# Attention and mixer on one core: the first block's relu and square in single tiles, relus of batch 0 on two engines, the last output tile in two column halves

## The chip, the cores and the metric

The kernel runs on one core of a Trainium2 chip. The metric is the device time of one execution in microseconds (us). A core has engines that run side by side and wait for each other through semaphores: TensorE (PE in the profile; its weight loads are listed as PEld), VectorE (DVE), ScalarE (ACT), GpSimd (POOL) and SyncE (SP), whose queue issues DMAs. Matmuls write to PSUM, in banks of 128 partitions x 512 columns of f32.

## The reference

For each of 8 batches, with 3008 tokens (S) and 256 channels:

```python
scores = (1.0 / S) * np.matmul(z, z.transpose(0, 2, 1))     # z: 8 x 3008 x 64
attn = np.maximum(scores, 0.0) ** 2
x = u * np.matmul(attn, v)                                  # u, v: 8 x 3008 x 256
h = np.maximum(x.transpose(0, 2, 1) @ w_tok1, 0.0) @ w_tok2 # 3008 -> 256 -> 3008
y = x + h.transpose(0, 2, 1)
out = y + np.maximum(y @ w_ch1, 0.0) @ w_ch2                # 256 -> 1536 -> 256
```

Every input is f32 and the output is f32; the kernel multiplies in bf16.

## The kernel before, in words

**Tiles.** Tokens are cut into 24 tiles of 128 (the last holds 64) and into six groups of four tiles, 512 tokens each (`QW`, `GK`; the last group has 448). For batch b, a block of queries q (512 tokens) and a group of keys g, the scores are made in two units (`pr` 0 and 1) of two key tiles each. `score_run` (L448) issues a unit's two matmuls into one pair of PSUM banks. `relu` (L480) scales and clips the pair on ScalarE and writes bf16 into a tile `at` (128 x 4 x 512), `square` (L509) squares it in place on VectorE. The product with v, attn @ v, accumulates over all key groups into `acc`, once for each half of the channels (`dh` 0 and 1).

**The first query block of batch 0** (`blk.whole`, q = 0) is done by `whole_matmul` (L596, matmuls at L609) with all 128 rows in one matmul; all other blocks go by `av_matmul` (L692) as two matmuls of 64 rows that run side by side. `grain` (L431) says in how many key tiles at a time a block is handed on: for the first two groups of (b, q) = (0, 0) a pair is used as soon as its square is done, through the events in `early`; later groups wait for all four tiles, through `blocks`.

**The ring.** Scores, turns and most other results share three pairs of PSUM banks (`RING = 3`; `take_slot`, `ring`). A slot comes back when its reader, for scores the relu, is done. In the first block `first_acc` (L358) keeps two further banks for the two sums.

**The planner.** The order of all engines' instructions is worked out when the kernel is built. A loop (L1743) keeps its own clock for TensorE (`pe[0]`) and for ScalarE, VectorE and SP (`free`). `push` (L364) queues an operation on an engine with the time when it is ready, the time that it keeps the engine busy, and the time after which its result counts; `run_engines` (L383) emits them in the order of their start. TensorE's next work is picked among scores, products with v and mixer pieces. While the first block is going and TensorE would have to wait, L1832 puts one matmul on zeros (`fill`, L202, L205) into each 0.22 of the planner's time. What is emitted is static: on the chip each engine keeps that order and waits where a result is late.

**The start** (L1532 on). z of batch 0 comes in f32 by six DMAs on SP and ScalarE's queues, v's first group by POOL (L223). Seven matmuls on zeros are issued, then for the first two groups of z VectorE casts (L178), TensorE turns four tiles by a matmul with the identity (L184) and ScalarE copies them out (L1716). POOL's next loads of v wait for the second of these copies (`after`, L124). One more matmul on zeros follows, and the planner's clocks are set by hand (5.3 for TensorE) before the first two units are scored. Groups 2 and 3 of z are turned by DMA (L150), 4 and 5 later on TensorE (`late_z`, L1638), as is the first group of u (`first_u`).

**The mixer** of a batch follows in pieces: token products (`tok1`, `tok2`), the first channel product (`ch1`, L1143, with relus at L1182 and L1184), and the second by seven products of a Strassen-like scheme (`product`, L1280) or plainly (`ch2`, L1366). **The end**: for the last group of the last batch `ch2` handles one tile at a time, in the order tile 2, the joint tile of two batches' last 64 rows, tile 0, tile 1. Each has 12 matmuls of 256 columns, then `residual` adds on VectorE (L1401), and SP issues the output DMA (L1404).

Of the kernel before, what the change touches and what calls it, by code (L numbers as in the profile page):

```python
# [57 lines left out]
def kernel(  # L58
# [143 lines left out]
    def fill(n, bank):  # L202

        for _ in range(n):
            nc.tensor.matmul(  # L205
                bank, zero[:, :P], zero[:], start=True, stop=True, skip_group_check=True)
# [157 lines left out]
    def push(engine, ready, busy, lat, fn, first=0, room=(), done=None, frees=()):  # L364
        op = Op(ready, busy, lat, fn, first, room, done, frees)
        waiting[engine].append(op)
        return op.done
# [62 lines left out]

    def grain(b, q, g):  # L431

        return 2 if b + q == 0 and g < 2 else GK
    turned = {}

    def can_score(first_unit, most):
# [11 lines left out]
    def score_run(us, start):  # L448
        for unit in us:
            (b, q, g), pr = unit  # L450
            zT = zTs[b].rearrange("p t s -> p (t s)")
            W = widths[q]
            slot, free_at = take_slot()
            begin = max(start, free_at, known(turned[b, q], turned[b, g]))
            cost = column_time(W)
            if triangle(b, q, g):

                cost = (column_time(QW), column_time(P))[pr]
            begin, start = on_pe(begin, "half", cost)
            sc = bank_pair(slot, "sc")  # L460
            for r, i, c0, c1 in parts(unit):
                k = z_tile(b, r, g * GK + i) * P
                m = z_tile(b, r, q * GK) * P
                h = slice(r * d_qk, (r + 1) * d_qk)
                nc.tensor.matmul(  # L465
                    sc[:, r, c0:c1], zT[h, k:k + P], zT[h, m + c0:m + c1],
                    start=True, stop=True)
            if pr == 0:
                live["at"] += 1
                at_free.pop(0)  # L470
            busy = 0.92
            if triangle(b, q, g):
                busy = (0.87, 0.43)[pr]
            if grain(b, q, g) < GK and pr == 0:
                early[b, q, g] = [Done() for _ in range(GK)]
            done = push("act", begin + cost + 0.21, busy, busy + 0.16,
                        lambda t, unit=unit, sc=sc: relu(unit, sc, t))
            ring.append((done, slot))

    def relu(unit, sc, t):  # L480
        (b, q, g), pr = unit
        W = widths[q]
        if pr == 0:
            ats[b, q, g] = sb.tile([P, GK * QW], BF16, tag="at", name="at", bufs=ROOM["at"])
            ready_at[b, q, g] = []
        at = ats[b, q, g]
        pair = slice(2 * pr, 2 * pr + 2)
        if triangle(b, q, g):
            a3 = at.rearrange("p (i w) -> p i w", w=QW)
            for r, i, c0, c1 in parts(unit):  # L490
                nc.scalar.activation(  # L491
                    a3[:, i, c0:c1], sc[:, r, c0:c1], ACT.Relu, scale=inv_S)
            push("dve", t, (0.62, 0.36)[pr], (0.76, 0.5)[pr],
                 lambda t: square_triangle(unit, t))
            return
        if flips(b, q, g):

            view = at.rearrange("p (j i s) -> p j i s", i=GK, s=P)[:, :, pair, :]
            sv = sc.rearrange("p i (j s) -> p j i s", s=P)
        else:  # L500
            view = at.rearrange("p (i w) -> p i w", w=QW)[:, pair, :W]
            sv = sc[:, :, :W]
        nc.scalar.activation(view, sv, ACT.Relu, scale=inv_S)  # L503
        ready_at[b, q, g].append(
            push("dve", t, 0.61, 0.75, lambda t: square(unit, view, t)))

    blocks = {}

    def square(unit, view, t):  # L509
        (b, q, g), pr = unit  # L510
        nc.vector.tensor_mul(view, view, view)  # L511
        if (b, q, g) in early:
            for e in early[b, q, g][2 * pr:2 * pr + 2]:
                e.t = t
            if pr == 0:
                blocks[b, q, g] = (
                    Done(t), ats[b, q, g].rearrange("p (i w) -> p i w", w=QW), "at", [1])
            else:
                ats.pop((b, q, g))
            return  # L520
        if pr < GK // 2 - 1:
            return
        at = ats.pop((b, q, g))
        uses = [1]
        if flips(b, q, g):
            uses[0] = 2
            attn = at.rearrange("p (j i s) -> p i j s", i=GK, s=P)
            done = push("sp", t, 2.2, 6.5, lambda t: flip(b, q, g, at, uses, done),
                        frees=fl_free,
                        room=lambda: has_room(("fl",)) and (  # L530
                            b < 2 or q or turned_back[b - 1] > 1))
        else:
            attn = at.rearrange("p (i w) -> p i w", w=QW)
        blocks[b, q, g] = (Done(t), attn, "at", uses)
        recent[0] = at[:, :1]
# [463 lines left out]
    def add_mixer(b):  # L999
# [347 lines left out]
        def fast(q):  # L1347

            return (b > 0 or q >= HALF) and (b, q) != (B - 1, NQ - 1)

        def ch2(q, half, i, end):
            apart = alone(q, half)
            if i == 0 or apart:
                st["o_slot"], _ = take_slot()
                st["op"] = bank_pair(st["o_slot"], "op")[:, 0, :].rearrange(
                    "p (i d) -> p i d", d=D)
# [79 lines left out]
        def alone(q, half):  # L1436

            return pieces_of(q, half) == 1 or (b, q, half) == (B - 1, NQ - 1, 0)
# [269 lines left out]
    for k, item in enumerate(items):  # L1708
        at_group(begin + k * (NQ * NG - NG - begin + 1 + W_LATER) // len(items), item)

    fill(7, bank_pair(0, "wp")[:, 0, :])

    for c in range(DT):
        zp = first_acc(c).rearrange("p (t s) -> p t s", s=P)
# [6 lines left out]
    load_u(0, 1)  # L1721
    for c in range(DT, GK):
        turn_first_z(c)
    fill(1, bank_pair(0, "wp")[:, 0, :])
    for c, t in enumerate([5.3, 5.9, 9.0, 10.0]):
        turned[0, c] = Done(t)
    pe[0] = 5.3
    free.update(act=5.75, dve=5.0, sp=7.0)
    score_run(units[:2], 5.3)
    late_z(4, 7.8)  # L1730
    late_z(5, 9.0)
    first_u(18.5)
# [152 lines left out]
```

## Time and profile before

| what | us |
|---|---|
| three runs, median (lowest, highest) | 1116.48 (1116.16, 1121.13) |
| the profiled execution's own time | 1116.06 |
| its span, first to last instruction | 1114.0 |
| TensorE busy, of the span | 1108.1 |
| VectorE, ScalarE, GpSimd busy | 780.5, 655.1, 162.7 |
| 8.3 to 24 us: VectorE, ScalarE busy, of 15.7 | 12.38, 14.23 |
| 24 to 60 us: VectorE, ScalarE busy, of 36 | 30.85, 34.82 |
| 60 to 100 us: VectorE, ScalarE busy, of 40 | 37.33, 36.80 |

The profile is one execution; its durations are compared with its own time, 1116.06, and that lies 0.4 below the median of the three runs. Matmuls overlap, and their ends are modelled: a single matmul of 512 columns is listed with 0.38 us, while a row of them start 0.22 apart. So the chain of waits, which goes from start to start, is the better measure of TensorE's time. In timeline lines, the first number is the start in us from the beginning of the span, the second the length of the merged group; in brackets stands the idle time before it and what ended it. "SPq" lines are issues of DMAs, not the transfers.

### The profile page before, as it was taken

The page shows a single profiled execution, that of the slowest core. Times are in us where ns is not written, and L with a number is a line of the kernel's source. Part 1 is how long each engine was busy: PE and PEld are TensorE (multiplying, and loading weights), DVE is VectorE, ACT ScalarE, POOL GpSimd, SP SyncE. Part 2 cuts the span into 40 slices and gives each one's busy share as a digit, 9 for nine tenths or more (in the row PEclk, how much of TensorE's full clock was granted, in tenths as well). Part 3 has the DMA queues.
Part 4 walks back from the last instruction along what each step waited for, and adds up shares of the span by engine and source line. Part 5 has one row for each costly group of instructions (what it writes and reads, how often), then busy time and mean ns, then how long its engine had stood idle before and what let it go on. Part 6 is the DMA issues. An engine that isn't in the chain of part 4 may idle for free.

```text
span 1114.0 us, 26933 instructions
## 1 busy us (share of the span) xinstructions
PE 1108.1 (99%) x10965; PEld 675.6 (61%) x10965; DVE 780.5 (70%) x1855; ACT 655.1 (59%) x817; POOL 162.7 (15%) x382
## 2 busy tenths in 40 slices
PE   9999999999999999999999999999999999999998
PEld 3444574666557665576555865557655576556676
DVE  6889846875758757588566885578756787557775
ACT  8999524645854458545675356653666536743354
POOL 5321100211003110031000311003200120000000
PEclk9999999999999999999999999999999999999999
DMA  9999955796987979779597897868968678585213
GB/s 178 173 183 157 208 117 114 124 179 135 183 137 142 187 126 185 142 141 209 128 174 132 143 197 144 168 121 158 191 156 172 109 157 174 128 160 99 63 58 95
DMA packets 466155, 165.51 MB, mean 149 GB/s; under 512 B 433072, under 2 KB 449008, under 8 KB 466032
## 3 DMA queue, kind: packets, MB, share of 16 engines
q1 hardware_dynamic: 436640, 131.11, 58.0%
q0 software_dynamic: 28880, 32.32, 20.6%
q8 instruction: 85, 1.39, 0.5%
q10 hardware_dynamic: 512, 0.38, 0.1%
q14 instruction: 38, 0.31, 0.1%
HBM read 65.40 MB, written 24.64 MB: 81 GB/s over the span
## 4 chain that ended last, share of the span: by engine, by line
PE 97%; DVE 1%; ACT 1%; issue 1%; POOL 0%; DVEq 0%; POOLq 0%; ACTq 0%
PE acc L692 41%; PE hp L1143 21%; PE xb L1280 10%; PE zb L1280 7%; PE sc L465 6%; PE h_ps L1086 4%; PE a_ps L1029 3%; PE op L1366 3%; PE first_acc L609 1%; DVE a_f L1045 0%; ACT h2pre L1182 0%; PE wp L205 0%; ACT at L503 0%; POOL hs L1156 0%; DVE at L511 0%
## 5 line engine op out<-in xcount | busy, mean ns | idle before, releaser
L1182 ACT ACTIVATE h2pre<-hp 128x1024 bf16<-128x1024 f32 (+1 forms) x277 | 269.4, 1007 | 257.8 <-PE hp L1143 165.3
L692 PEld LDWEIGHTS <-v_sb 64*128 64x128 bf16 x4418 | 238.0, 94 | 219.3
L692 PE MATMUL acc<-at,v_sb 64*128 64x512 bf16 (+1 forms) x2738 | 338.8, 374 | 0.0
L503 ACT ACTIVATE at<-sc 128x1024 bf16<-128x1024 f32 (+1 forms) x290 | 287.5, 1027 | 72.2 <-PE sc L465 65.4
L511 DVE TENSOR_TENSOR at<-at 128x1024 bf16<-128x1024 bf16 (+1 forms) x290 | 198.5, 687 | 110.7 <-ACT at L503 106.7
L1143 PE MATMUL hp<-xT,w_ch_sb 128*128 128x512 bf16 (+1 forms) x1152 | 273.5, 375 | 0.1
L692 PE MATMUL acc<-fl,v_sb 64*128 64x512 bf16 (+1 forms) x1680 | 191.4, 367 | 0.0
L1143 PEld LDWEIGHTS <-w_ch_sb 128*128 128x128 bf16 x1152 | 106.2, 98 | 99.8 <-issue 3.0
L465 PE MATMUL sc<-zT 64*128 64x512 bf16 (+1 forms) x732 | 131.3, 360 | 0.1
L1280 PEld LDWEIGHTS <-hsum 128*128 128x128 bf16 x1944 | 115.9, 98 | 17.6 <-issue 1.1
L1280 PEld LDWEIGHTS <-h2pre 128*128 128x128 bf16 x1458 | 89.1, 98 | 19.3 <-issue 1.2
L820 ACT COPY cp<-acc 128x512 f32<-128x512 f32 (+1 forms) x94 | 54.9, 584 | 71.4 <-PE acc L692 59.8
L826 DVE TENSOR_TENSOR cp<-acc,cp 128x512 f32<-128x512 f32 (+1 forms) x94 | 63.5, 675 | 42.3 <-ACT cp L820 41.8
L491 ACT ACTIVATE at<-sc 128x512 bf16<-128x512 f32 (+3 forms) x152 | 56.1, 444 | 45.4 <-PE sc L465 45.0
L1223 DVE TENSOR_TENSOR hsum<-h2pre 128x512 bf16<-128x512 bf16 (+1 forms) x132 | 52.2, 400 | 37.7 <-ACT h2pre L1182 35.9
L1280 PE MATMUL xb<-w_mix_sb,hsum 128*128 128x128 bf16 x972 | 68.6, 219 | 0.4 <-DVE ro L1317 0.3
L542 DVE TENSOR_TENSOR at<-at 128x512 bf16<-128x512 bf16 (+3 forms) x152 | 41.5, 321 | 38.3 <-ACT at L491 38.2
L1317 DVE TENSOR_TENSOR ro<-xb,u_sb 128x256 f32<-128x256 f32 (+1 forms) x132 | 52.6, 399 | 21.9 <-PE xb L1280 20.2
L465 PEld LDWEIGHTS <-zT 64*128 64x128 bf16 x732 | 42.0, 94 | 41.8 <-issue 3.8
L124 POOL CAST mark<-at 128x1 f32<-128x1 bf16 x24 | 8.9, 369 | 375.2 <-DVE at L511 375.2
L846 DVE TENSOR_TENSOR xT<-cp,uT 128x512 bf16<-128x512 f32 (+1 forms) x94 | 62.4, 664 | 0.8
L1095 DVE TENSOR_TENSOR xT<-xT,h_ps 128x1024 bf16<-128x1024 bf16 (+1 forms) x48 | 54.6, 1172 | 4.7 <-PE h_ps L1086 4.6
(89 smaller groups left out, 983.0 us busy)
## 6 DMA issues: line engine op xcount, KB each, us to landing
out_dram<-ro SPq DMA_DIRECT2D x37, 512.0 KB, 2.9
v_sb<-in_v_dram POOLq DMA_DIRECT2D x40, 256.0 KB, 4.6
ur<-in_u_dram POOLq DMA_DIRECT2D x40, 256.0 KB, 5.1
w_tok_sb<-in_moe_w_tok_dram POOLq DMA_DIRECT2D x10, 256.0 KB, 10.7
zs<-in_z_dram POOLq DMA_DIRECT2D x35, 64.0 KB, 3.7
at<-at SPq DMA_TRANSPOSE x114, 2.4
out_dram<-ro SPq DMA_DIRECT2D x7, 256.0 KB, 2.2
fl<-at SPq DMA_TRANSPOSE x105, 4.4
```

What stands on the lines that cost most here:

```text
L465: nc.tensor.matmul(sc[:, r, c0:c1], zT[h, k:k + P], zT[h, m + c0:m + c1], start=True, stop=True)
L491: nc.scalar.activation(a3[:, i, c0:c1], sc[:, r, c0:c1], ACT.Relu, scale=inv_S)
L503: nc.scalar.activation(view, sv, ACT.Relu, scale=inv_S)
L511: nc.vector.tensor_mul(view, view, view)
L692: nc.tensor.matmul(o, vs[blk.b, g][rows, i, dh * P:(dh + 1) * P], rhs, start=(dh, h) not in blk.begun, stop=stop, skip_group_check=True)
L820: nc.scalar.copy(cp[:, :W], acc[:, 1, :W])
L826: nc.vector.tensor_add(cp[:, :W], acc[:, 0, :W], cp[:, :W])
L846: nc.vector.tensor_mul(xT[:, dh, :full * P].rearrange("p (t s) -> p t s", s=P), acc[:, :full * P].rearrange("p (t s) -> p t s", s=P), uT[: ...
L1095: nc.vector.tensor_add(to, to, h[:, :, :n * P].rearrange("p h (s t) -> p h t s", t=n))
L1143: nc.tensor.matmul(hps[r % len(hps)][:, r, :W], w_ch1_sb[:, dc, cc * P:(cc + 1) * P], xT[:, dc, :W], start=(dc == 0), stop=(dc == DT - 1))
L1182: nc.scalar.activation(h2[:, :, :W], hp[:, :, :W], ACT.Relu)
L1280: nc.tensor.matmul(to[:, i * P:(i + 1) * P], lhs, weights[:, c2, :], start=(first_use and c2 == 0 and i == 0), stop=(c2 == CHT // 2 - 1), ...
```

## The change

There are three parts. At the start, six matmuls on zeros are issued instead of seven and the single one after the turns is left out; the planner's clocks are set 0.5 lower. For the first key group of the first query block the first pair's relu and square are done in two instructions each, one for each key tile, and the products follow tile by tile (`grain` 1). For batch 0, relus of groups that are handed on whole may go to VectorE, as one multiply-and-max from PSUM, where the planner's queues say that ScalarE would be done later than VectorE with relu and square (0.92 against 1.76). As relus can now change order, `at` is made by whichever pair comes first, and a block is done when both pairs are squared. At the end, tile 1 of the last group is computed in two halves of 128 columns, each with 12 matmuls, a bank of its own, an add and an output DMA.

```diff
@@ -430,7 +430,7 @@
     def grain(b, q, g):
-        return 2 if b + q == 0 and g < 2 else GK
+        return GK if b + q or g > 1 else 1 + g
@@ -473,14 +473,25 @@
             if grain(b, q, g) < GK and pr == 0:
                 early[b, q, g] = [Done() for _ in range(GK)]
-            done = push("act", begin + cost + 0.21, busy, busy + 0.16,
-                        lambda t, unit=unit, sc=sc: relu(unit, sc, t))
+            if grain(b, q, g) == 1 and pr == 0:
+                busy += 0.14
+            ready = begin + cost + 0.21
+            engine = "act"
+            if b == 0 and grain(b, q, g) == GK:
+                def load(e):
+                    return max(free[e], ready) + sum(op.busy for op in waiting[e])
+                if load("act") + 0.92 > load("dve") + 1.76 + ON_DVE:
+                    engine, busy = "dve", 1.15
+            done = push(engine, ready, busy, busy + 0.16,
+                        lambda t, unit=unit, sc=sc, engine=engine: relu(unit, sc, engine, t))
             ring.append((done, slot))
 
-    def relu(unit, sc, t):
+    ON_DVE = 0.0
+
+    def relu(unit, sc, engine, t):
         (b, q, g), pr = unit
         W = widths[q]
-        if pr == 0:
+        if (b, q, g) not in ats:
...
-        nc.scalar.activation(view, sv, ACT.Relu, scale=inv_S)
+        if grain(b, q, g) == 1 and pr == 0:
+            for i in range(2):
+                nc.scalar.activation(view[:, i], sv[:, i], ACT.Relu, scale=inv_S)
+                push("dve", t + 0.5 * (i - 1), 0.34, 0.5,
+                     lambda t, i=i: square_one(unit, view, i, t))
+            return
+        if engine == "act":
+            nc.scalar.activation(view, sv, ACT.Relu, scale=inv_S)
+        else:
+            nc.vector.tensor_scalar(view, sv, inv_S, 0.0, AX.mult, AX.max)
...
+    def square_one(unit, view, i, t):
+        (b, q, g), pr = unit
+        nc.vector.tensor_mul(view[:, i], view[:, i], view[:, i])
+        early[b, q, g][i].t = t
+        if i == 0:
+            blocks[b, q, g] = (
+                Done(t), ats[b, q, g].rearrange("p (i w) -> p i w", w=QW), "at", [1])
...
-        if pr < GK // 2 - 1:
+        squared[b, q, g] = squared.get((b, q, g), 0) + 1
+        if squared[b, q, g] < GK // 2:
             return
@@ -1348,8 +1377,32 @@
+        def last_tile(q, half, i, end):
+
+            res = sb.tile([P, 2, D], F32, tag="fl", name="res", bufs=ROOM["fl"])
+            k = half * 2 + i
+            for h in range(DT):
+                slot, _ = take_slot()
+                op = bank_pair(slot, "op")[:, 0, :P]
+                for cc in range(CHT):
+                    nc.tensor.matmul(
+                        op, st["h2", q, cc // 4][:, cc % 4, k * P:(k + 1) * P],
+                        w_ch2_sb[:, cc, h * P:(h + 1) * P], start=(cc == 0), stop=(cc == CHT - 1))
+
+                def residual(t, h=h, op=op):
+                    nc.vector.tensor_add(res[:, h, :P], op, st["u", q][:, h, k, :])
+                    nc.sync.dma_start(
+                        out=rows_of(out[b], q)[:, k, h * P:(h + 1) * P], in_=res[:, h, :P])
+
+                ring.append((push("dve", end - 0.65 * (1 - h) + 0.21, 0.21, 0.36, residual), slot))
+            done_with_h2(q)
+            release("us", us_uses[q])
+
         def ch2(q, half, i, end):
             apart = alone(q, half)
+            if (b, q, half, i) == (B - 1, NQ - 1, 0, 1):
+                last_tile(q, half, i, end)
+                return
@@ -1708,7 +1761,7 @@
-    fill(7, bank_pair(0, "wp")[:, 0, :])
+    fill(6, bank_pair(0, "wp")[:, 0, :])
...
-    fill(1, bank_pair(0, "wp")[:, 0, :])
-    for c, t in enumerate([5.3, 5.9, 9.0, 10.0]):
+    for c, t in enumerate([4.8, 5.4, 9.0, 10.0]):
         turned[0, c] = Done(t)
-    pe[0] = 5.3
-    free.update(act=5.75, dve=5.0, sp=7.0)
-    score_run(units[:2], 5.3)
+    pe[0] = 4.8
+    free.update(act=5.25, dve=4.5, sp=7.0)
+    score_run(units[:2], 4.8)
```

More of the change, by code (lines that the diff above doesn't have):

```diff
@@ L502, in relu @@
             sv = sc[:, :, :W]
-        nc.scalar.activation(view, sv, ACT.Relu, scale=inv_S)
+        if grain(b, q, g) == 1 and pr == 0:
[8 more added lines that the diff above has]
+            nc.vector.tensor_scalar(view, sv, inv_S, 0.0, AX.mult, AX.max)
         ready_at[b, q, g].append(
             push("dve", t, 0.61, 0.75, lambda t: square(unit, view, t)))
-    blocks = {}
+    blocks, squared = {}, {}
+    def square_one(unit, view, i, t):
[5 more added lines that the diff above has]
+                Done(t), ats[b, q, g].rearrange("p (i w) -> p i w", w=QW), "at", [1])
     def square(unit, view, t):
```

## The prediction

> **What bounds the kernel now.** I read the page first: the span and the engines' busy shares, then the chain that ended last.
>
> ```profile
> span 1114.0 us, 26933 instructions
> ...
> PE 1108.1 (99%) x10965; PEld 675.6 (61%) x10965; DVE 780.5 (70%) x1855; ACT 655.1 (59%) x817; POOL 162.7 (15%) x382
> ...
> PE 97%; DVE 1%; ACT 1%; issue 1%; POOL 0%; DVEq 0%; POOLq 0%; ACTq 0%
> ```
>
> TensorE (PE) is on the chain for 97% of the span. A microsecond is gained only where TensorE waits or works for nothing. The table by windows of 100 us shows 99.64 to 100 us of PE busy from 200 on; between 200 and 1090 its idle time adds up to 1.2 us. What is left lies at the two ends. Next view: the chain in order of time, first 10 us (start, length, what).
>
> ```profile
> 1.20 3.17 PE wp L205 x7
> 4.36 0.85 PE first_acc L184 x8
> 5.21 0.44 PE wp L205
> 5.66 0.04 issue
> 5.70 0.98 PE sc L465 x4
> 6.68 0.75 PE first_acc L205 x3
> 7.43 0.54 PE sc L465 x4
> 7.97 0.54 PE first_acc L205 x2
> 8.51 0.86 PE first_acc L609 x4
> 9.37 0.22 PE zp L184 x4
> ```
>
> L205 is a matmul on zeros. Seven stand ahead of the first turns of z, one behind them, and five (3 and 2) pass time until the first product with v (L609) can start, at 8.35 by the timeline. From there the chain is useful matmuls without a gap. The third view is the timeline of the other engines at that place.
>
> ```profile
> 6.35 1.02 ACT L503 ACTIVATE at<-sc 128x1024 bf16<-128x1024 f32 x1 [0.45 <-PE sc L465]
> ...
> 7.40 0.69 DVE L511 TENSOR_TENSOR at<-at 128x1024 bf16<-128x1024 bf16 x1 [2.67 <-ACT at L503]
> ...
> 10.81 0.23 PEld L609 LDWEIGHTS <-v_sb 128*128 128x128 bf16 x2 [0.21 <-DMA v_sb<-in_v_dram]
> ```
>
> The first L609 waits for relu (6.35 to 7.37) and square (7.40 to 8.09). At 10.81 PE's weight load waits for a load of v. The last view is the timeline of SP and VectorE at the end (SP's lines are DMA issues).
>
> ```profile
> 1108.45 0.33 SPq L1404 DMA_DIRECT2D out_dram<-res  x1
> 1108.88 0.51 SPq L1404 DMA_DIRECT2D out_dram<-res  x1
> 1109.48 0.54 SPq L1404 DMA_DIRECT2D out_dram<-res  x1
> 1110.12 0.54 SPq L1404 DMA_DIRECT2D out_dram<-res  x1
> 1111.07 0.34 SPq L1404 DMA_DIRECT2D out_dram<-res  x1
> ...
> 1110.62 0.42 DVE L1401 TENSOR_TENSOR res<-op,u_sb 128x256 f32<-128x256 f32 x1 [0.89 <-PE op L1366]
> ```
>
> The last matmul ends at 1110.58, its residual at 1111.04, the last DMA is issued at 1111.07 and takes 1.7 us to land.
>
> **Part 1, two matmuls on zeros fewer.** A zero matmul ahead of 6 us takes 3.17 minus its tail over 7: starts lie 0.43 apart. Six end at 1.20 + 6 x 0.43 = 3.76. The first turn then waits for the cast of z (3.29 plus 0.43) and a weight load of 0.10, so it starts at 3.88, not 4.16: 0.28 earlier. The eighth zero matmul (0.44) lay beside ScalarE's cast (4.83, 0.58), for which the scores wait at 5.57; taking it away gains nothing by itself. The scores start at 5.42 instead of 5.70. What is late next is ScalarE's cast, and then the relu: 6.07 instead of 6.35.
>
> **Part 2, relu and square tile by tile.** By the nearest rows a 128x512 relu takes 0.60 (L491), two 128x512 casts in a row start 0.48 apart (L1716), and a 128x512 square takes 0.42 (L542). So tile 0 is squared at 6.07 + 0.60 + 0.03 + 0.42 = 7.12, tile 1 at about 7.57. Two instructions instead of one cost ScalarE 2 x 0.48 against 0.92 from relu to relu, at least 0.04, at most the 0.14 that the planner books. But the first v, issued at 1.43, takes 6.3 us to land: 7.73. No product can start earlier. Nor does the order let it: in the planner's own clock (4.80 + 0.095 + two scores = 5.33) the next two scores can go when the first bank is nearly free, at 6.22, so (6.22 - 5.33)/0.22 gives four zero matmuls between, where there were three; the two behind the second pair of scores go. TensorE then runs: scores to 6.3, zeros to 7.35, a change of shape (0.1, as 0.54 for four scores against 0.43), scores to 7.88, 0.1, first product at 7.98. That is 0.37 ahead of 8.35.
>
> The lead isn't kept whole. After the eight matmuls of the first block, one turn of z and two more scores TensorE comes to the second v at about 10.65. It now lands at 6.08 + 4.7 = 10.8. Its issue on POOL follows ScalarE's second cast, so it moves 0.28 earlier, with four more loads of v behind it on the same queue; if the 4.7 hold it lands at 10.5, and if the queues' traffic holds it at 10.8, the lead ends there. So the start is worth 0 to 0.37; I take **0.3**, since the issue is 0.28 earlier and the row's duration is the only evidence of what follows. Behind the waiting weight load stand the scores of the fourth block and ScalarE for them, which has two relus (about 10.3 to 12.2) to do first, so that wait isn't handed on. The later loads land well ahead of use (the third at about 12.1, used after 13.7). Once TensorE never waits, the lead goes to the end unchanged.
>
> **Part 3, relus on VectorE.** Such a relu has no row with a multiply; the nearest is L1184, 128x1024 from PSUM, 1.22 on VectorE, against 1.03 on ScalarE. The rule takes VectorE when ScalarE's queue plus 0.92 exceeds VectorE's plus 1.76; of three scores issued together the third can qualify. It shortens no wait of TensorE, since there is none in batch 0 after 8.35. What it may cost is cover: in 8.3 to 24 VectorE is busy 12.38 of 15.70, and three such relus (3.67) would bring it to 16.05, 0.35 over; in 24 to 60 there is room for four (30.85 of 36), in 60 to 100 for two (37.33 of 40). The rule compares queues, so a full VectorE gets none, and finished blocks ahead of TensorE cover a late one. Value 0, bounds -0.4 (a bank freed sooner saves two changes of shape of 0.1 each, twice) and +0.35.
>
> **Part 4, the last tile in halves.** TensorE: 24 matmuls of 128 columns for 12 of 256. L1280's twelve take 0.67 on the chain, so 1.34 for 1.31: +0.03. VectorE's last add is 128x128: 0.29 (L1317) for 0.42: -0.13. But SP now issues two DMAs where there was one. The fourth issue ends at 1110.66; half 0 is ready at 1109.11 + 0.67 + 0.2 + 0.3 = 1110.3 and stands right behind it, from about 1110.72. The three issues that stood directly behind another took 0.51 to 0.54, the two that didn't 0.33 and 0.34. Half 1, ready at 1110.96, is therefore issued at 1111.12 to 1111.35, not 1111.07, and its own issue may take 0.2 more. Landing follows: 1.7 for 128 KB here and 2.0 for 64 KB of 64 rows, so half the bytes save 0.1 at most. Bounds -0.05 and +0.5; I take **+0.25**, towards the rows of issues that queue.
>
> **Sum.** -0.3 + 0 + 0.25 = -0.05. The profiled execution took 1116.06 (span 1114.0 and 2.1 around it); the three other runs have a median of 1116.48 (1116.16 to 1121.13). I forecast against the median: **1116.4**, which is no change. A measurement of this kernel tells about 0.5% (5.6 us) from no change.
>
> [...] The rows first: zero matmuls start 0.43 apart up to 6 us and 0.22 apart from 6.6 on; turns of z take 0.85 for eight at 4.36 and 0.22 for four at 9.37. TensorE runs at half pace for its first 5 us, though the granted clock of that window reads 1.00. [...]
>
> **Rivals.**
> - *The fast pace comes late (slower).* Place: TensorE now idles from 4.73 to 5.42, 0.7 us, where it idled 0.3 (5.44 to 5.70). By the rows the fast pace came some 5.1 us after the first matmul (1.20 to 6.3). If the longer gap starts that count afresh at 5.42, it comes at 10.5, and the matmuls from 6.3 on do in 4.2 us the work of 2.1. The four zeros are in it and only pass time ahead of v at 7.73, which absorbs about 0.5. Price 1.6: **1118.0**. It decides when the scores at 7.4 still start 0.43 apart. For it: the gap is new and longer. Against: TensorE is still busy for most of 1.2 to 6.3. Chance 0.12. [...]
> - *The second v lands early and the order has fewer gaps (faster).* The lead of 0.37 stays whole, batches of scores save 0.4 in changes of shape, SP's issues take 0.34 (end +0.05) and some of the later 1.2 us of idling goes: -0.35 - 0.4 + 0.05 - 0.4 = -1.1, **1115.4**. For it: relus on VectorE free banks sooner, and the whole later order is planned anew. Chance 0.25.
> - *VectorE or the new order costs more (slower).* 0.35 in the first block and as much idling again as the 1.2 us now seen: **1118.0**. The point: squares in 8 to 24 that wait for VectorE and not ScalarE, with L609 behind them. Chance 0.13.
> - *The VectorE branch is never taken:* then part 3 is 0 anyway, and the forecast stands.
>
> **How the numbers follow.** The forecast, within 0.6 of 1116.4, has 0.50. To hold the time 8 times in 10 the range takes in most of the three rivals: 1114.7 to 1118.2. All cases lie within 5.6 us of the median; for an order that goes wrong over hundreds of microseconds I leave faster 0.02, same 0.94, slower 0.04.
>
> **What would show it.** Part 1: first turn at 3.88, scores at 5.42, one group of L205 of six. Part 2: relus of 128x512 at 6.07, four zeros behind the first scores, first L609 at about 8.0, and L609 of the second block at 10.5 to 10.8, with PE's weight load waiting for v there. Part 3: some lines of VectorE at<-sc with 128x1024 from f32, no wait of PE for VectorE. Part 4: six L1404-like issues, the last at 1111.1 to 1111.4 less the lead. I'd be wrong if the lead at 24 us were over 0.6 or below 0, if the fast pace came late, or if PE's idle time between 200 and 1090 left 0 to 2.4.

## The result, and the profile after

| | before | after |
|---|---|---|
| median of 22 runs each, us | 1116.59 | 1120.6 |
| lowest, highest | 1115.44, 1121.13 | 1118.05, 1130.78 |
| the profiled execution | 1116.06 | 1121.0 |
| its span | 1114.0 | 1119.1 |

The ratio after to before is 1.0046, with a 95% interval of 1.0029 to 1.0063. A second set of runs gave 1119.3 against 1116.88, ratio 1.0042 (1.0025 to 1.0059). So the change costs 2.4 to 4.0 us by the medians, and some 5 by the ratios, in which the longest runs weigh more. That is within the 0.5% which the prediction called no change, but outside its range, which ended at 1118.2. Nine of the ten longest runs of after have a mean granted clock of 0.998 or lower, as have 11 of the 32 in both sets and 4 of 111 runs of before.

The page of after first: the span, the busy line and the chain that ended last.

```profile
span 1119.1 us, 26955 instructions
...
PE 1109.2 (99%) x10974; PEld 680.1 (61%) x10974; DVE 782.5 (70%) x1858; ACT 654.9 (59%) x817; POOL 161.1 (14%) x382
...
PE 92%; DVE 4%; DMA 2%; ACT 1%; issue 0%; DVEq 0%; ACTq 0%
```

TensorE's share of the chain fell from 97% to 92%; DMA has entered it with 2%, and VectorE has gone from 1% to 4%. The chain in order of time (start, length, what) shows where the DMA comes in.

```profile
1.20 2.74 PE wp L205 x6
...
3.97 0.62 PE first_acc L184 x4
...
4.61 0.59 ACT zT L1769
...
5.25 0.63 PE sc L465 x2
...
5.91 0.11 ACT at L516
6.02 6.49 DMA zT<-zr
...
12.55 0.60 PE sc L465 x4
```

Up to 5.91 this is the start that was forecast: six zeros, the first turn at 3.97, the scores at 5.25. Then a DMA takes the chain for 6.49 us: the second DMA transpose of z (`turn_first_z`, L150), issued at 6.02 and landed at 12.51. In before it was issued at 5.84 and had landed at 10.63. The timeline at that place:

```profile
5.91 1.08 ACT L516 ACTIVATE at<-sc 128x512 bf16<-128x512 f32 x2 [0.22 <-PE sc L465]
6.54 0.91 DVE L531 TENSOR_TENSOR at<-at 128x512 bf16<-128x512 bf16 x2 [1.62 <-ACT at L516]
7.94 1.47 PE L638 MATMUL first_acc<-at,v_sb 128*128 128x512 bf16 x6
...
11.49 0.60 PE L638 MATMUL first_acc<-at,v_sb 128*128 128x512 bf16 x2 [0.78 <-DMA v_sb<-in_v_dram]
12.55 0.60 PE L465 MATMUL sc<-zT 64*128 64x512 bf16 x4 [0.46 <-DMA zT<-zr]
```

The relus in single tiles (L516) and their squares (L531) are in time, and the first product with v (L638, L609 before) starts at 7.94, not 8.35. Then TensorE waits twice, for the second load of v (landed at 11.45, before 10.77) and for the transpose. The two waits take 0.95 and 0.62 out of its row of starts.

To see where the rest comes from, I follow the lag: by how much a landmark that both kernels have (a VectorE gate, a copy out of PSUM) comes later in after than in before, and how much longer than usual the next matmul is in starting.

| where (us in after) | lag added | what TensorE waits for |
|---|---|---|
| up to 8 | -0.4 | nothing; the lead |
| 10.7 to 12.6 | +1.57 | v's second load (0.95), z's transpose (0.62) |
| 8 to 40 | +0.5 | 28 changes between matmuls of 64 and of 128 rows in the first 240 us, 22 in before; starts lie 0.31 apart at a change and 0.22 in a row, so about 0.1 each; one of the six falls into the wait at 12.55 |
| 110.8 | +0.7 | scores: a PSUM bank that ScalarE's relu frees late |
| 132.9 and 150.8 | +0.8 | VectorE (at 150.8 an add, L1436, which had waited 4.3 for an output DMA to land; 3.3 in before) |
| 494, 630, 768 | +0.8 | the sums `hsum`, VectorE |
| behind the last matmul | +1.1 | SP's output DMAs |
| sum | 5.1 | span 1119.1 against 1114.0 |

These are differences of single executions. pe_longer and sp_longer, further down, run before's program up to its end, and yet they lag behind before's trace by 0.2 at 65 us and by 1.5 from 126 us on. So much a trace can differ by itself.

SP's issues at the end of after, which stand against the five of before:

```profile
1112.44 0.33 SPq L1457 DMA_DIRECT2D out_dram<-res  x1
...
1113.47 1.63 SPq L1457 DMA_DIRECT2D out_dram<-res  x1
...
1115.83 0.40 SPq L1394 DMA_DIRECT2D out_dram<-res  x1
...
1114.64 0.29 DVE L1393 TENSOR_TENSOR res<-op,u_sb 128x128 f32<-128x128 f32 x1 [0.38 <-PE op L1388]
```

The third issue, a store of 64x256 that stands ahead of the halves, takes 1.63; the same one took 0.54 in before. The fourth follows at 1115.20, and the halves (L1394) queue behind it: the last result is ready at 1114.93 and its DMA is issued at 1116.32.

### The profile page after: what moved, and what is told of

Same layout as the page of the kernel before. It is cut to its first block, busy times and chain, and to the rows that moved or that the text cites. A ratio compares the mean times of both kernels' runs of the same rounds, so it can differ in the third digit from the quotient of the medians.

```text
span 1119.1 us, 26955 instructions
## 1 busy us (share of the span) xinstructions
PE 1109.2 (99%) x10974; PEld 680.1 (61%) x10974; DVE 782.5 (70%) x1858; ACT 654.9 (59%) x817; POOL 161.1 (14%) x382
## 4 chain that ended last, share of the span: by engine, by line
PE 92%; DVE 4%; DMA 2%; ACT 1%; issue 0%; DVEq 0%; ACTq 0%
PE acc L721 40%; PE hp L1172 20%; PE xb L1309 9%; PE zb L1309 7%; PE sc L465 6%; PE h_ps L1115 4%; PE a_ps L1058 3%; PE op L1419 2%; DMA out_dram<-ro 1%; PE first_acc L638 1%; ACT at L521 1%; DVE at L539 1%; DMA zT<-zr 1%; DVE ro L1346 1%; DVE a_f L1074 0%
## 5 line engine op out<-in xcount | busy, mean ns | idle before, releaser
L721 PEld LDWEIGHTS <-v_sb 64*128 64x128 bf16 x4418 | 243.2, 94 | 214.9 <-issue 0.4
L521 ACT ACTIVATE at<-sc 128x1024 bf16<-128x1024 f32 (+1 forms) x287 | 284.1, 1026 | 74.6 <-PE sc L465 67.3
L1172 PEld LDWEIGHTS <-w_ch_sb 128*128 128x128 bf16 x1152 | 106.1, 98 | 100.7 <-issue 4.2
```

What stands on the lines that cost most here:

```text
L721: nc.tensor.matmul(o, vs[blk.b, g][rows, i, dh * P:(dh + 1) * P], rhs, start=(dh, h) not in blk.begun, stop=stop, skip_group_check=True)
L1172: nc.tensor.matmul(hps[r % len(hps)][:, r, :W], w_ch1_sb[:, dc, cc * P:(cc + 1) * P], xT[:, dc, :W], start=(dc == 0), stop=(dc == DT - 1))
```

## The experiments

**Theory A:** the two zeros fewer let v's second load be issued ahead of z's second transpose, and the two get into each other's way; the rest is the end and changes of shape. **Rivals:** the order of the work, planned anew, costs by itself (B: through the two relus that went to VectorE; C: through any new order); the end is the halves' own doing, or SP's longer queue. Every kernel below has a profile, and its time is compared with before on the same chip. "Lag" is that behind before's trace.

| kernel | median us (runs) | ratio to before, 95% | lag at 65 us | lag at TensorE's end | added behind it |
|---|---|---|---|---|---|
| after, second set | 1119.3 (10) | 1.0042 (1.0025 to 1.0059) | +1.4 | +2.1 | +1.0 |
| v_later | 1119.62 (12) | 1.0028 (1.0007 to 1.0049) | +0.8 | +2.2 | +1.3 |
| v_sooner | 1117.43 (12) | 1.0002 (0.9989 to 1.0015) | +0.6 | +0.4 | 0.0 |
| zeros_alone | 1117.28 (12) | 1.0003 (0.9984 to 1.0022) | +0.8 | +1.2 | 0.0 |
| end_alone | 1117.16 (12) | 1.0000 (0.9983 to 1.0018) | +0.4 | +6.5 | +0.5 |
| tiles_alone | 1116.19 (12) | 1.0006 (0.9992 to 1.0019) | 0.0 | -0.5 | 0.0 |
| no_dve | 1124.84 (6) | 1.0082 (1.0067 to 1.0098) | -0.3 | +3.3 | +1.3 |
| end_undone | 1118.34 (12) | 1.0022 (1.0006 to 1.0038) | +1.3 | +1.7 | 0.0 |
| after_mended | 1117.67 (11) | 1.0012 (0.9996 to 1.0027) | +0.4 | +1.0 | +0.5 |
| tiles_mended | 1118.12 (11) | 1.0007 (0.9996 to 1.0018) | +1.2 | +1.1 | +0.4 |
| relu_on_act | 1120.19 (11) | 1.0033 (1.0015 to 1.0051) | +2.3 | +2.4 | +0.6 |
| pe_longer | 1117.08 (10) | 1.0005 (0.9993 to 1.0017) | +0.2 | -0.2 | +0.5 |
| sp_longer | 1117.93 (1) | | 0.0 | +1.5 | its own load |
| held_whole | 1117.67 (11) | 1.0017 (1.0000 to 1.0034) | +0.5 | +0.7 | 0.0 |

Before had medians of 1116.35 to 1116.88 in these sets.

### The start: four kernels on the loads

**v_later** is after, with a small memset on GpSimd ahead of v's loads; **v_sooner** is before, with v's loads waiting for the first copy of z, not the second; **zeros_alone** is before with two zeros fewer and nothing else; **end_alone** is before with the last tile in halves.

```diff
     after(zTs[0][:, DT * GK - 1, :1])
+    nc.gpsimd.memset(w_tok1_sb[:, 0:2, :], 0.0)        # v_later
```
```diff
-    after(zTs[0][:, DT * GK - 1, :1])                  # v_sooner
+    after(zTs[0][:, GK - 1, :1])
```
```diff
-    fill(7, bank_pair(0, "wp")[:, 0, :])               # zeros_alone
+    fill(6, bank_pair(0, "wp")[:, 0, :])
...
-    fill(1, bank_pair(0, "wp")[:, 0, :])
```

> The changed kernel, with one memset of 128x512 on POOL (of a weight tile that is loaded later) between POOL's wait for ScalarE's second cast and the loads of v, so that the second load of v is issued some 0.4 us later, at about 6.3 us. Theory A (the earlier load of v shares the DMA engines with the two transposes of z that run at the same time, and both land late): the second transpose lands before 11 us instead of 12.5, v at 10.7 to 11.0 instead of 11.45, the scores of the fourth group of keys start at about 11 instead of 12.55; the median falls from 1120.6 to about 1119 and the scatter of 13 us over the runs shrinks to about 3. Rival B (the new order of the matmuls costs the time, not the landings): the median stays within 0.5 of 1120.6.

> The kernel before, with one edit: POOL's loads of v wait for ScalarE's first cast instead of its second, so that the second load of v is issued about 0.4 us sooner (5.6 instead of 6.08); the order of the matmuls is that of before. Theory A: the transposes and the load collide here too; the second transpose lands after 11.5 instead of 10.63, v no sooner than 10.8; the median rises by 1 to 2.5 us to 1117.6 to 1119, with a wider scatter. Rival B: no change, 1116.6 within 0.4, or 0.1 to 0.3 faster since v is there sooner.

> The kernel before with only the two matmuls on zeros taken out (six and none); the planner's clocks and so all other instructions are those of before. The scores start at 5.3 to 5.4. Theory A: v is issued 0.2 to 0.3 us sooner and may collide: between 0 and +2 us, 1116.6 to 1118.6, with some runs high. Prediction: -0.3 to 0. Rival C (the longer gap on TensorE holds its half pace for longer): scores at about 7.1 still start 0.43 apart, +1 us or more in the runs where it happens, with a mean granted clock below 1.000.

> The kernel before with only the last tile in two halves of 128 columns. Theory D (SP's issues stand in a queue and are late): the last issue starts 0.3 to 1.5 us later after the last matmul, the span ends 0.3 to 1.1 us later, median 1116.9 to 1117.7. If the late third issue of the changed kernel's profile (1.63 us) was chance: +0.1 to +0.5. If the halves hide VectorE's add as meant: -0.1.

The landings settle the start. The two issues of before and of after, from the timelines of SP and GpSimd:

```profile
5.84 1.23 SPq L150 DMA_TRANSPOSE zT<-zr  x1
...
6.08 0.76 POOL L223 DMA_DIRECT2D v_sb<-in_v_dram  x1
```
```profile
6.02 1.21 SPq L150 DMA_TRANSPOSE zT<-zr  x1
...
5.87 0.76 POOL L223 DMA_DIRECT2D v_sb<-in_v_dram  x1
```

In before the transpose is issued 0.24 ahead of v, in after 0.14 behind it. Over all sixteen traces (later kernels included):

| kernel | v issued after the transpose by | transpose landed | v landed |
|---|---|---|---|
| v_sooner | -0.60 | 12.26 | 10.30 |
| no_dve | -0.19 | 11.90 | 11.30 |
| zeros_alone | -0.16 | 12.24 | 11.64 |
| end_undone, relu_on_act, after (second) | -0.15 | 12.10, 12.11, 12.29 | 11.67, 11.30, 11.66 |
| after | -0.14 | 12.51 | 11.45 |
| sp_longer, tiles_mended | +0.04, +0.06 | 10.80, 11.51 | 10.87, 11.41 |
| end_alone | +0.10 | 10.62 | 11.23 |
| held_whole, after_mended, pe_longer | +0.14, +0.15, +0.16 | 10.74, 10.50, 10.80 | 10.60, 10.73, 10.86 |
| before, tiles_alone | +0.24, +0.25 | 10.63, 10.16 | 10.77, 10.90 |
| v_later | +0.31 | 10.90 | 11.11 |

With v issued first, the transpose landed at 11.90 to 12.51 in all seven; with the transpose first, at 10.16 to 11.51 in all nine. From its issue the load takes 4.9 to 5.9 in the seven and 4.7 to 5.4 in the nine, so for v the two groups overlap. What decides is the order of the two issues and not v's own time: after_mended and held_whole issue v at 5.91, earlier than zeros_alone (5.94), but behind the transpose. The DMA packets show it too: in before SP's queue moves 514 of its packets from 7.5 to 8 us, and v's queue has 65 packets in the half microsecond from 8; in after SP's queue drops to 33 and 54 packets in the two half microseconds from 7.5, and then gets about 110 in each half microsecond from 8.5 to 10.5, beside 97 to 118 of v's.

The price is the lag: zeros_alone, with 2 zeros fewer and nothing else, is 0.14 ahead at 4.8 us and 0.75 behind from 22 us on. v_sooner shows it with all zeros in place. Both times agree with no change within their intervals, which a loss of 0.4 to 1.2 fits; v_sooner's 1117.43 is below the 1117.6 to 1119 that was expected, and its v landed at 10.30, sooner than expected. In v_later the collision is gone, but its lead was lost to the first v, which landed at 8.57 in that execution (7.66 in after). Its runs didn't come closer together, as A expected: they still lie 12 us apart (1117.4 to 1129.28). So the collision isn't what spreads them.

end_alone's own part, at the end, is 0.5. Its trace holds something else, a wait of 2.6 at 106 us; that is taken up below.

### Which part of the order

**no_dve** is after with no relu on VectorE, **end_undone** after with the last tile whole, **tiles_alone** before with only the relu and square in single tiles; after was run again beside them.

```diff
-    ON_DVE = 0.0                                       # no_dve
+    ON_DVE = 1e9
```
```diff
-            if (b, q, half, i) == (B - 1, NQ - 1, 0, 1):   # end_undone
-                last_tile(q, half, i, end)
-                return
```
```diff
-        return 2 if b + q == 0 and g < 2 else GK       # tiles_alone: with relu, square_one
+        return GK if b + q or g > 1 else 1 + g
```

> The kernel after, with no relu of batch 0 on VectorE (the rule never chooses it; the order of the work is planned anew without these two). Theory A (the second load of v and the transposes of z collide, worth about 1 us, the end and the changes of shape the rest): only two relus are concerned, so it stays at 1119.5 to 1121, with transposes and v landing at 11.5 or later as in the kernel after. Theory B (the order planned with VectorE's relus costs the stalls at 107 to 150 us): these waits go, the lag at 160 us is 1.0 and not 2.5 to 3.3, the median falls to 1117.5 to 1118.5. Theory C (any new order meets such stalls): waits in other places, the same sum, 1119 to 1121.

> The kernel after, with the last token tile whole, as before. If the halves at the end cost what the traces show there (0.5 to 1.1 us from the last matmul to the end): 0.3 to 1.1 below the kernel after, 1119.4 to 1120.3; span minus end of TensorE's work falls from 4.5 to 3.4. If the end costs nothing on the whole (as its single trial against the kernel before hinted, 1117.2 against 1116.9): within 0.3 of the kernel after.

> The kernel before with the first relu and square tile by tile alone (eight matmuls on zeros and the planner's first clocks as before, no relus on VectorE, the last tile whole). Theory A (loads collide): the load of v is issued when it was before, so transposes land near 10.6 and v near 10.8, no wait over 0.3 there, and the time is 1116 to 1117. Theory C (the order planned anew costs by itself, by changes of shape and waits at 107 to 150 us): 1118 to 1119.5, lag of over 1 by 160 us although the start is level.

> The kernel after once more, beside the others: 1119 to 1121.5. If the stalls at 107 to 150 us belong to its order, they stand at the same lines in this second trace; if they belong to single executions, they stand elsewhere or are gone, while the late landing of the transposes of z (12.5) and of v (11.5) stays.

tiles_alone, as A expected, is level: its transposes land at 10.16 and its lag is 0.0 from 48 to 600 us. The first product comes at 7.79, 0.56 ahead, but the second v (10.90) takes that back. So part 2 neither gains nor costs by itself.

Behind its last matmul end_undone takes as long as before, where the kernel with halves takes 1.0 more, and its median is 1.0 lower than that of after in the same set, though the two intervals overlap. By the traces the end is worth 1.0 of the loss.

no_dve refutes B as it was put. Taking the two relus off VectorE made the kernel slower, 1124.84, over six runs, four of them with a mean granted clock of 0.998 or lower. Its start is better (20 changes of shape in the first 240 us in place of 28, lag -0.3 at 65 us, in spite of a late transpose), but it loses 3.6 from there to the end. The row of TensorE in the list of who waited for whom, 60 to 140 us (us in total, times, longest), and the chain at 103 to 113 show the waits and the place of the last one:

```profile
PE sc L465 <- ACT at L521: 2.6, 4, 0.9
```
```profile
103.22 8.34 DMA fl<-at
...
111.67 1.03 ACT at L521
...
112.75 0.39 PE sc L465 x2
```

The first three of the four waits, at 78.8, 89.2 and 90.1 us (1.7 in sum), are scores that wait for a relu to free their bank. In the last, at 112.7, a relu (ScalarE, L521) waits for a buffer `at`, which a DMA transpose (`flip`, L591) still reads; TensorE's scores wait for the relu. In no_dve's order the first of these transposes is issued at 91.7 us, behind a third `x_pair`; in before at 85.7. So all six `at` buffers are taken here, and a queue on SP that runs some microseconds later comes out at TensorE. That is the wait which after meets at 110.8 too (0.7; the transpose landed at 109.60), and end_alone (2.6), whose order at this place is that of before. The second trace of after doesn't have it: 0.0 there (the transpose landed at 108.14), 0.8 at 150 us. So both orders have the place, and whether it bites is a matter of the single execution. That the new order adds to this wait isn't shown. A seventh buffer wasn't tried.

### Putting the parts right

**after_mended** holds v's load back by a memset, and stores the first half from ScalarE's queue; **tiles_mended** does the same to tiles_alone with two zeros fewer and the last tile in halves; **relu_on_act** keeps after's planned order, but runs the two relus on ScalarE; **sp_longer** is before with one DMA more behind the last store.

```diff
     after(zTs[0][:, DT * GK - 1, :1])
+    nc.gpsimd.memset(w_tok1_sb[:, 0:1, :], 0.0)        # after_mended, tiles_mended
...
-                    nc.sync.dma_start(
+                    (nc.scalar, nc.sync)[h].dma_start(
```
```diff
-            nc.vector.tensor_scalar(view, sv, inv_S, 0.0, AX.mult, AX.max)   # relu_on_act
+            nc.scalar.activation(view, sv, ACT.Relu, scale=inv_S)
```
```diff
+    nc.sync.dma_start(out=mark[:, 4:], in_=rows_of(z[0], 0)[:, 0, 4:32])     # sp_longer
```

> The kernel after, with a small memset ahead of v's five loads on GpSimd's queue (the second load of v is issued near 6.1 us, as in the kernel before, not at 5.8 to 5.9) and the first half of the last tile stored from ScalarE's queue instead of SP's. Theory A (an issue of v ahead of some point between 5.94 and 6.08 puts it in the way of z's transposes): second transpose landed by 10.9, second v by 11.2, TensorE's waits at 10 to 13 us gone, lag at 40 us +0.3 (a lead of 0.3 less the changes of shape, 0.5 to 0.75) instead of 1.3 to 1.6. Theory of the end (SP's longer queue): third store at the end 0.54 instead of 1.5 to 1.8, span within 0.3 of what the kernel before has behind its last matmul. Together 1117.0 to 1118.0. If the start's loss is the new order's and not the loads', the lag at 40 us stays above 1.

> The kernel before with the tile-by-tile relu and square, the two zero matmuls fewer, the second load of v held to about 6.1 us by a small memset, and the last tile in halves stored from two queues; the planner's first clocks as before and no relus on VectorE. If the three losses found (loads that collide, an order that puts more changes of shape and waits, SP's queue at the end) are all there is: nothing is lost, lead of 0.3 at 10 us, level or up to 0.4 ahead at 40 us, end 0 to 0.2 shorter, median 1116.2 to 1116.9, at or a little below the kernel before. If the rest of the change costs by itself: 1117.5 or more.

> The kernel after in its planned order, but the two relus that the rule gave to VectorE run on ScalarE at the same places of the order. If running them on VectorE is what costs (VectorE late for its squares): lag at 40 us down by 0.3 or more. If the order that was planned for them costs, not where they run: lag at 40 us 1.3 to 1.9 as in the kernel after, TensorE's 22 changes of shape as there, median 1119 to 1121. If VectorE's relus helped (a bank freed sooner): up to 0.5 worse than the kernel after.

> The kernel before with one small load more on SP, behind the last store (it loads 128x28 of z into an unused place, and lengthens the end by itself). In every kernel with the last tile in halves the third of SP's last stores took 0.98 to 1.79, in every one without 0.54, though it stands ahead of the halves. If the cause is that SP's stream of instructions is longer (by code that is still to come): the third store takes 0.9 to 1.8 here too. If the cause is the halves themselves (their size, their adds): it takes 0.54.

after_mended came out as expected at the start: transpose at 10.50, v at 10.73, lag +0.4 at 65 us instead of 1.4 to 1.6. In TensorE's order of after, a load that is issued 0.15 behind the transpose, and not 0.15 ahead of it, gives about 1.1 of the loss back. The median fell to 1117.67.

tiles_mended missed: 1118.12, lag 1.2. In its trace the first v lands at 8.66, and TensorE waits 1.5 for it. Over the sixteen traces the first v lands at 7.63 to 8.66, though its issue doesn't move; no run here shows what it depends on.

relu_on_act is 0.7 to 0.9 worse than after at 65 us, in the same order of TensorE's work: the difference arises at 21.4 us. So in these traces the two relus on VectorE help the order that was planned for them, and where they run isn't what costs. The order is what is left.

The end wasn't mended: a long issue of 1.37 (the fourth, in after_mended) stands there all the same, though SP has one DMA fewer than in after, and sp_longer's five stores keep 0.33 to 0.54 with one more (its lag, +1.5, comes at 126 us, from a wait for ScalarE). So SP's queue isn't the cause. In relu_on_act it is the fourth issue as well, with 1.16.

### The end

All kernels with halves had one more packet in the page's row for queue 8, by its name the fetch of instructions. The row of before:

```profile
q8 instruction: 85, 1.39, 0.5%
```

Each packet has 16384 bytes. The last one comes 11.7 us ahead of TensorE's end in before, and 1.3 in after (at 1113.30, beside the store that takes 1.63). **pe_longer** is before with twelve small matmuls behind the last one; **held_whole** is after with v held back and the last tile whole. Until these two, the cause of the end's cost was open.

```diff
+            if (b, q, half, i) == (B - 1, NQ - 1, 0, 1):                     # pe_longer
+                spare = bank_pair(st["o_slot"], "op")[:, 1, :8]
+                for _ in range(12):
+                    nc.tensor.matmul(spare, ident[:], ident[:, :8], start=True, stop=True,
+                                     skip_group_check=True)
```

> The kernel before (last tile whole) with twelve small matmuls (128x8, on the identity, result unused) behind the last real one, so that TensorE's stream has 24 instructions more, as with the last tile in halves. In every kernel with halves one block of instructions of 16 KB more is fetched (86, not 85), 0.5 to 1.7 us ahead of TensorE's end, and one of SP's last issues takes 0.98 to 1.79 instead of 0.54. If the longer stream of TensorE is the cause: 86 blocks here too, the last within 2 us of TensorE's end, and one of SP's last issues takes 0.9 or more, though the tile is whole; the span's end is later by what it delays, up to 1. If the halves themselves are the cause: all of SP's last issues are 0.33 to 0.54.

> The kernel after with v's second load held to about 6 us by a small memset, and the last tile whole. What is left of the change is the lead at the start, the tile-by-tile relus and the order planned anew with two relus on VectorE. If the three losses named are all (loads 1.0 to 1.2, order 0.5 to 0.75 in changes of shape plus waits up to 0.8 near 110 and 150 us, end 0.5 to 1.1): lag +0.3 to +0.5 at 65 us, end as before, 1116.9 to 1117.7. If there is a loss that hasn't been found: 1118 or more.

pe_longer's row for that queue, and SP's issues:

```profile
q8 instruction: 86, 1.41, 0.5%
```
```profile
1109.25 1.26 SPq L1409 DMA_DIRECT2D out_dram<-res  x1
...
1110.60 0.54 SPq L1409 DMA_DIRECT2D out_dram<-res  x1
```

The tile is whole, SP's program is that of before, and the third issue takes 1.26. So it is the length of TensorE's stream: 24 instructions more (12 matmuls with their weight loads) need one more block, which is fetched just when the last stores are issued. In nine traces with 86 blocks one of SP's last issues took 0.98 to 1.79; in seven with 85 none took over 0.54. It adds 0.4 to 1.3 behind the last matmul. The small matmuls run from 1110.86 on, behind the long issue, so they didn't stretch it themselves. Fetches elsewhere meet long issues too (one of 1.09 at 1050.9 in after): of the 42 issues of stores on SP that take over 0.7 in the sixteen traces, 37 have a fetch on queue 8 in the 0.6 ahead of their start or during it. Other issues beside a fetch stay at 0.33 to 0.66. How a fetch holds an issue up, no run here shows.

held_whole has a lag of +0.5 at 65 us and +0.7 at the end, which is the smallest of the kernels with after's order, 28 changes of shape included. Its trace holds no loss that wasn't named. Its median, 1117.67, is 1.3 above before's, more than the trace explains.

No kernel was measurably faster than before. tiles_alone, whose median is 0.7 lower, has an interval on both sides of 1.

## Why the prediction was wrong

**Part 1, the zeros: right in its own time, wrong in what it moved.** First turn at 3.97 (forecast 3.88, though its terms 3.29 + 0.43 + 0.10 add up to 3.82), scores at 5.25 (5.42), six zeros in one group. The step that failed is "if the 4.7 hold it lands at 10.5, and if the queues' traffic holds it at 10.8". The load took 5.6 from issue to landing, and the bound was on the wrong side: 11.45. The prediction weighed v's queue against itself. It didn't ask what v's load passes by being earlier: z's second transpose on SP, whose issue, 0.24 ahead of it in before, didn't move with it (6.02 in after, 5.84 in before). The term for the start was -0.3; what was measured is -0.4 for the lead and +1.57 for the two waits.

**The rival "the fast pace comes late" didn't happen.** From the first of four scores (7.41) to the next product (7.94) 0.53 pass in after, and 0.54 (7.43 to 7.97) in before. The trace's record of the granted clock starts, at 1.00, at 6.49 in before, about where starts 0.43 apart give way to starts 0.22 apart, and at 6.69 in after; ahead of that it holds nothing, so the 1.00 read for the first 5 us says nothing of them. Over the sixteen traces it starts at 4.24 (v_sooner) to 7.11 (after's second). The first four scores take 0.61 in v_sooner (from 5.27), 0.98 in before (from 5.70) and 1.03 in after's second trace (from 5.20), so the moment of the fast pace changes from one execution to the next.

**Part 2: right.** Relus at 5.91 (6.07), four zeros behind the first scores, first product at 7.94 (7.98). That v's first load lands at 7.7 was one trace's number; the others have up to 8.66, and in after's second trace, with 8.16, the first product starts at 8.20. So the closeness of 0.04 is in part luck.

**Part 3: right that few relus would qualify (two, at 13.2 and 18.2 us, 1.22 each) and that VectorE has room for them; wrong that the value is 0.** The bounds, -0.4 to +0.35, looked at where the relus run. The order that comes out of the planner has a cost that the term put at nothing: six changes of shape more (+0.5), in every trace of after's order. With the collision and the halves taken away, held_whole is left with a lag of 0.7 and a median 1.3 above before's, with an interval that begins at no change. At 110, 133 and 150 us waits of 0.1 to 0.8 reach TensorE as well; but end_alone (2.6 at 106), sp_longer (1.25 at 125.9) and zeros_alone (0.4 at 148.8) meet such waits in before's order, so the traces don't show that they come from the new one. The sentence "Once TensorE never waits, the lead goes to the end unchanged" failed with it: the page showed TensorE without idle time in 200 to 1090 us, not with time to spare.

**Part 4: right that SP's issues queue and that this costs, wrong in size:** +1.1 and 1.0 in after's two traces, for a term of +0.25 with +0.5 as its upper bound. The rows of issues that queue, 0.51 to 0.54, were the right rows for SP; one more block of TensorE's instructions isn't among them.

**The rival that came nearest** was "VectorE or the new order costs more", with 1118.0 and 0.13: its place (squares that wait for VectorE in 8 to 24 us) was wrong, its other half, idling again in the later order, was right.

Of the 5.1 in the profiled execution, shown by taking it away and back: the loads, 1.0 to 1.2 (after_mended, held_whole, and zeros_alone and v_sooner the other way); the end, 1.0 (end_undone; pe_longer brings 0.5 of it about). Seen in traces only: changes of shape 0.5, waits at 110 to 150 us up to 1.5. Of the single waits at 494 to 768 us, +0.8, only this trace tells. Open is what takes runs of after to 1130, which its profiles don't show. The runs tell which part it goes with. A mean granted clock of 0.998 or lower is found in 26 of 95 runs of the kernels with two zeros fewer and an order planned anew for that start (after, v_later, no_dve, end_undone, after_mended, relu_on_act, held_whole), and in 5 of 158 runs of those with before's order (before, v_sooner, zeros_alone, end_alone, pe_longer, sp_longer); tiles_alone has 2 of 12, tiles_mended none of 11. So it goes with that order; after_mended and held_whole, without the collision of loads, still have 3 of 22. A drop of the granted clock after a wait of TensorE is the candidate: end_alone's profile, with a mean of 0.998, has one, where TensorE waits from 106.1 to 108.7. The table by windows there (stretch, length, busy time of the engines, then granted clock, DMA share and GB/s):

```profile
105.00:109.50 4.50, 2.10 (x21) 1.00 (x18) 1.63 (x5) 1.87 (x3) 0.00 (x0) 1.00 1.19 194
109.50:112.90 3.40, 3.40 (x20) 1.50 (x16) 2.16 (x4) 2.02 (x4) 0.53 (x1) 0.50 1.35 238
```

From 109.5 the granted clock is 0.50 for 3.413 us by the clock's own record, and then 1.00 again. On the chain two scores take 0.43 in that stretch (at 110.30) and 0.22 behind it (at 113.81). The 102.4 us that the record has at 1.00 ahead of the drop are 30 times 3.413, and the last of the thirty, 106.09 to 109.50, holds the whole wait. In before and after the record at 1.00 lasts 1109.33 and 1112.75 us, up to a 0.50 behind the last instruction: 325 and 326 times that length, so in these three traces it changes in such steps. The lag goes from +0.4 at 73 us to +6.7 at 131: waits of 4.3 (2.6 the longest) and 1.7 for the half pace. None of after's profiles caught such a drop, so for after's longest runs this is argued, not shown; and that the wait of 2.6 brought the drop about is the author's estimate from this one trace.

## What to carry to other kernels

When work is taken out ahead of a load, list what that load now passes on the other queues, and look at issue times and not at durations: an issue that went from 0.24 behind a transpose to 0.14 ahead of it put off both landings, by 1.9 and by 0.7 us. An order that a planner makes anew is a change of its own: count its changes of shape (28 for 22 here, about 0.1 us each), and look for places where a late transfer reaches the full engine, before giving it the value 0. Instructions added to a full engine can cost behind its end: pe_longer's 24 more on TensorE took the fetched blocks from 85 to 86, the last one fell beside the last stores, and the span's end came 0.5 later behind the last real matmul.

## What the hardware did that was not expected

One block of 16 KB of TensorE's instructions, fetched near the end, stretched an issue of a store on SP from 0.54 to between 0.98 and 1.79 us in nine traces; pe_longer, with nothing else added, has 1.26 for 0.54.

A load of v on GpSimd's queue and a DMA transpose on SP's landed 4.7 and 4.8 us after their issues in before. With the load issued first, by as little as 0.14, the transpose took 6.49 (after), and the load 5.6.
